# Converting float64 weights on the chip: from a float addition to an integer addition

## The chip, the cores and the metric

One core of a Trainium2 chip runs the whole program. Its engines are TensorE (PE, with its weight loads shown apart as PEld), VectorE (DVE), ScalarE (ACT), GpSimd (POOL) and SyncE (SP), which here only issues DMAs. The metric is the time of one execution in microseconds (us), the median of several runs.

## The reference

Three layers follow one another in float32. The weights of the second, `moe_w_in` and `moe_w_out`, are drawn in float32 and divided by a numpy scalar, and reach the kernel as float64.

```
a  = softmax over (keys within 16 of the query, and 24 block maxima + log 32)   # attention, 4 x 8 x 768 x 64
x  = (a @ [v, block means of v]) as 3072 tokens x 512
h  = x @ w_in                    # 512 x 2048, float64 in memory
x  = (h * cos(h)) @ w_out        # 2048 x 512, float64 in memory
logits = x @ phi                 # soft mixture: 8 experts x 4 slots
out = softmax_rows(logits) @ experts(softmax_columns(logits).T @ x)
```

## The kernel before

**Blocks and slots.** The 3072 tokens are six blocks of 512. The middle layer's 2048 hidden columns are sixteen tiles of 128. The main loop has a slot `s` for each hidden tile `f = s % 16` of each block, 96 slots. In a slot, `mm1` (L384 to L386) forms the hidden tile `h` with 12 products of 128 x 512, `act1` and `act2` (L400 to L411) turn it into `h cos h`, and `mm2` (L423 to L425), two slots later, adds 12 products to the block's four accumulators. Each float32 operand is split into a high part and a rest, so one product is three: `split_w` does so for the weights (L372 on ScalarE, L373 on GpSimd), L410 and L411 for the hidden tile, L362 and L363 for attention's result. The hidden tile has two places in PSUM, so slot `s + 2` writes over that of `s`, and must wait until L407 has read it.

**The cosine.** VectorE takes the hidden tile modulo one turn (L400, L401), ScalarE forms the sine of that (L402), VectorE multiplies (L407), ScalarE and GpSimd split (L410, L411).

**The weights.** A tile `f` of `w_in` and `w_out` together is 128 x 1024 float64 numbers, 1 MB as pairs of 32-bit words. `load_w(f)` brings it into `raw[f]`. There are two places for it (the first three tiles have a place more), so `load_w(f + 2)` waits on SP until all readers of `raw[f]` are done, and other loads stand behind it in SP's queue. Three steps then make the float32 tile `W[f]`, times 256, which stays in memory for all six blocks:

- `conv_1`: ScalarE multiplies the upper word, read as a float, by 2^-111 and takes its absolute value (L123).
- `conv_2`: VectorE shifts this three bits to the left (L134), puts in the sign (L135), takes the sign and exponent alone into a second tile `cv` (L137) and multiplies that by the lower word times 2^-52 (L138).
- `conv_3`: GpSimd adds `cv` to `W[f]` (L143).

The tile `cv` has two places by turns: one for odd `f` and one for even. Tiles 0 to 3 are converted ahead of the main loop, among the first block's attention (the tokens c0 to c3 of the string `PRE` say where). Tiles 4 to 15 are converted in slots 0 to 11, each three slots before its first split. So the conversion lies in the first block alone; the other five blocks find their weights ready.

**What sets the order.** Each engine runs its instructions in one order. The program is written out slot by slot, with attention's steps for later blocks put between (`at`, `at2`), and a planner that simulates a time line (`schedule_with_timeline_sim`) then fixes the order on each engine.

Of the kernel before, what the change touches and what calls it, by code (L numbers as in the profile page):

```python
# [23 lines left out]
QB = 64                      # queries per attention block  # L24
NQ = S // QB                 # 12 blocks per head
WIN, SUMB = 16, 32
KL = QB + 2 * WIN            # local keys of a block's window
NSUM = S // SUMB
KC = KL + NSUM               # key columns of a block: local and summary
NP = B * H // 2              # head pairs  # L30
TB = 512                     # tokens of a MoE block
# [37 lines left out]
SCALE = 1.0 / math.sqrt(D)    # a power of two  # L69
W_SCALE = 256.0              # the weights are held times this  # L70
TWO_PI = float(np.float32(2.0 * math.pi))
MAGIC = 12582912.0           # 1.5 * 2**23: adding and subtracting it rounds to an integer
# [3 lines left out]
def body(ctx: ExitStack, tc: tile.TileContext, q0, qk, kT, vn, vx, w, phi, ex, cst, out):  # L76
# [41 lines left out]
    def conv_1(f):  # L118
        """float64 words to the nearest float32, times 256: the upper word as a float, times 2^-111, has the
        exponent's offset adjusted; three bits to the left its exponent and 20 mantissa bits are in place;  # L120
        the sign follows, and the lower word is added as a float."""
        W[f] = wres.tile([128, 2, 512], F32, name=f"w{f}", tag=f"w{f}")
        nc.scalar.activation(W[f], raw[f][:, :, :, 1].bitcast(F32), AF.Abs, scale=2.0 ** -111)  # L123

    cvt = {}

    def conv_2(f):
        hw, lw = raw[f][:, :, :, 1], raw[f][:, :, :, 0]
        hw, lw = (x.rearrange("p a c -> p (a c)") for x in (hw, lw))
        wf = W[f].rearrange("p a c -> p (a c)")  # L130
        wi_ = wf.bitcast(I32)
        pool, tag = (wres, "w15") if f % 2 and f < 15 else (att, "cv")
        t = cvt[f] = pool.tile([128, 1024], F32, name=f"cv{f}", tag=tag, bufs=1)
        nc.vector.tensor_single_scalar(out=wi_, in_=wi_, scalar=3, op=ALU.logical_shift_left)  # L134
        nc.vector.scalar_tensor_tensor(out=wi_, in0=hw, scalar=-0x80000000, in1=wi_,  # L135
                                       op0=ALU.bitwise_and, op1=ALU.bitwise_or)
        nc.vector.tensor_single_scalar(out=t.bitcast(I32), in_=wi_, scalar=-0x00800000, op=ALU.bitwise_and)  # L137
        nc.vector.scalar_tensor_tensor(out=t, in0=lw.bitcast(U32), scalar=2.0 ** -52, in1=t,  # L138
                                       op0=ALU.mult, op1=ALU.mult)

    def conv_3(f):
        wf = W[f].rearrange("p a c -> p (a c)")
        nc.gpsimd.tensor_tensor(out=wf, in0=wf, in1=cvt.pop(f), op=ALU.add)  # L143

# [5 lines left out]
    def bank(name):  # L150
        """ahead of the main loop the accumulators' banks serve too"""
# [23 lines left out]
    def load_vb(b, i):  # L175
        """a third of a batch's values; the first batch's go into space that is not in use yet"""
# [12 lines left out]
    def vsum(b, i):  # L189
        """means of 32 keys: a pair's in its 32 rows"""  # L190
# [8 lines left out]
    def vsum_first():  # L199
        """the first batch's, all pairs in the rows that follow a window's keys"""  # L200
# [37 lines left out]
    def first_A(g, j):  # L238
        """scores of the first block's groups: the mask, times 8, is the last product of the sum"""
# [73 lines left out]
    def att_exps(g):  # L313
        """the same by row: the bias subtracts the maximum, the accumulator sums"""
# [6 lines left out]
    def att_norm(g, eng=None):  # L321
        # the hidden layer is formed in turns: x leaves attention divided by 2 pi
# [198 lines left out]
    def grab(pool, tag, units=1, **kw):  # L521
        """A freed place for expert weights: the next units are loaded there."""
# [38 lines left out]
    def fill(n):  # L561
        """products of no use: the tensor engine's clock halves when it idles"""
# [49 lines left out]
    for b in range(1, B):  # L612
        s = 8 * (3 * b - 2) - 4      # before the batch's first group
# [22 lines left out]
    def sched_m2(j, s):  # L636
# [4 lines left out]
        e = 2 * s + HF[1] + OX       # with the attention's exponentials  # L641
# [53 lines left out]
    def cT_mm(j):  # L695
        """the tokens' weights, transposed, four times"""
# [7 lines left out]
    def cT_split(j):  # L704
        """the high part and the rest, twice"""
# [63 lines left out]
    kept = []  # L769

    def release(u, want):
        """the place that an expert unit held goes to other use up to a number, else to the next units"""
# [36 lines left out]
    # the second products and the output by halves of the columns: the first half leaves while the second is formed  # L809
# [3 lines left out]
    for h in range(2):  # L813
# [23 lines left out]
        for i in range(NB):  # L837
            pool, tag, kw = places[(NB * h + i) % 4]
            o = pool.tile([128, 4, 256], F32, name=f"o{h}_{i}", tag=tag, **kw)
            for t in range(2):  # L840
# [7 lines left out]
                if i == 1:  # L848
                    before = slot_out, product   # what the other half's products leave room for
# [73 lines left out]
```

## Time and profile before

| | us |
|---|---|
| median of 3 runs | 809.73 (809.7 to 812.68) |
| span of the profiled execution, first to last instruction | 807.5 |
| TensorE busy in the span | 763.4 |
| VectorE busy | 516.0 |
| GpSimd busy | 465.7 |
| ScalarE busy | 422.0 |

The profile has one execution, with no time of its own beside its span. The median lies 2.2 us above that span. Busy time is the union of an engine's instructions; a group's sum over its instructions can be a little larger, since the end of one and the start of the next overlap. The mean granted clock of TensorE over the span is 0.976 of 2.4 GHz.

### The profile page before, as it was taken

The numbers are of one execution on the slowest core, as the hardware profiler recorded it, in microseconds if no ns is written. First come the engines' busy times: TensorE is split into PE (matmuls) and PEld (weight loads), VectorE is DVE, ScalarE is ACT, GpSimd is POOL, SyncE is SP. The second block draws the span as 40 slices with busy tenths as digits, with TensorE's granted clock in tenths as the row PEclk, the third lists the DMA queues.
The fourth block names the chain that finished last, engine by engine and source line by source line (L and its number), as shares of the span: only waits on it lengthen the run. The fifth ranks groups of instructions, "written<-read, shape, count | busy, mean of one in ns | idle before, by whom it ended". The sixth has DMA issues, their size and how long they took to land.

```text
span 807.5 us, 13934 instructions
## 1 busy us (share of the span) xinstructions
PE 763.4 (95%) x5517; PEld 590.9 (73%) x5517; DVE 516.0 (64%) x715; ACT 422.0 (52%) x774; POOL 465.7 (58%) x321
## 2 busy tenths in 40 slices
PE   9976788899999999999999999999999999999994
PEld 8865565667777877888778877778777888877453
DVE  5599999987746757557457369476476444433623
ACT  4839454754645645546537456565475454734212
POOL 1556999997655755745655646647547666562000
PEclk9997998999999999999999999999999999999998
DMA  9955555403233012011121110120000753227988
GB/s 317 308 159 212 218 177 181 168 25 109 68 99 105 3 52 72 25 63 64 52 63 38 50 56 21 50 76 25 25 1 27 275 195 102 79 88 277 364 308 271
DMA packets 34673, 98.30 MB, mean 122 GB/s; under 512 B 3376, under 2 KB 13744, under 8 KB 32560
## 3 DMA queue, kind: packets, MB, share of 16 engines
q1 hardware_dynamic: 34608, 97.42, 35.5%
q8 instruction: 43, 0.70, 0.4%
q14 instruction: 22, 0.18, 0.1%
HBM read 89.15 MB, written 6.29 MB: 118 GB/s over the span
## 4 chain that ended last, share of the span: by engine, by line
PE 68%; DVE 19%; ACT 5%; issue 4%; DMA 3%; POOL 0%; SPq 0%; ACTq 0%; DVEq 0%
PE h L384 9%; PE acc L423 9%; PE h L385 8%; PE acc L425 8%; PE h L386 8%; PE acc L424 8%; PE sc L286 3%; DVE w L135 3%; PE av L353 2%; DVE cv L137 2%; PE yp L822 2%; PE hp L789 2%; PE tr L335 2%; PE xt L449 2%; DVE cv L138 2%
## 5 line engine op out<-in xcount | busy, mean ns | idle before, releaser
L373 POOL TENSOR_TENSOR wol<-w,woh 128x512 fp32r<-128x512 f32 x96 | 141.4, 1473 | 100.5 <-ACT woh L372 100.4
L373 POOL TENSOR_TENSOR wil<-w,wih 128x512 fp32r<-128x512 f32 x96 | 136.1, 1418 | 71.7 <-ACT wih L372 71.7
L384 PE MATMUL h<-xh,wih 128*128 128x512 f32 x384 | 158.0, 411 | 13.9 <-DVE a L407 13.9
L411 POOL TENSOR_TENSOR gl<-a,gh 128x512 fp32r<-128x512 f32 x96 | 130.9, 1365 | 62.8 <-ACT gh L410 60.4
L385 PE MATMUL h<-xl,wih 128*128 128x512 f32 x384 | 155.3, 404 | 1.8 <-DVE xl L363 1.8
L386 PE MATMUL h<-xh,wil 128*128 128x512 f32 x384 | 154.9, 403 | 0.5 <-POOL wil L373 0.5
L423 PE MATMUL acc<-woh,gh 128*128 128x512 f32 x384 | 151.9, 402 | 0.5 <-DVE x L444 0.5
L425 PE MATMUL acc<-woh,gl 128*128 128x512 f32 x384 | 146.8, 399 | 5.2 <-POOL gl L411 5.2
L424 PE MATMUL acc<-wol,gh 128*128 128x512 f32 x384 | 150.6, 395 | 0.0
L400 DVE TENSOR_SCALAR a<-h 128x512 f32<-128x512 f32 x96 | 65.7, 685 | 85.5 <-PE h L386 81.6
L402 ACT ACTIVATE a<-a,halfpi 128x512 f32<-128x512 f32 x96 | 69.5, 724 | 96.2 <-DVE a L401 94.4
L372 ACT CAST wih<-w 128x512 fp32r<-128x512 f32 x96 | 59.3, 618 | 87.9 <-PE h L385 71.8
L407 DVE TENSOR_TENSOR a<-h,a 128x512 f32<-128x512 f32 x96 | 66.1, 689 | 59.3 <-ACT a L402 59.1
L384 PEld LDWEIGHTS h<-xh,wih 128*128 128x128 f32 x384 | 74.4, 194 | 32.8 <-DVE a L407 16.1
L425 PEld LDWEIGHTS acc<-woh,gl 128*128 128x128 f32 x384 | 71.9, 189 | 23.3 <-POOL gl L411 6.4
L385 PEld LDWEIGHTS h<-xl,wih 128*128 128x128 f32 x384 | 74.4, 194 | 17.7 <-DVE xl L363 2.3
L386 PEld LDWEIGHTS h<-xh,wil 128*128 128x128 f32 x384 | 74.2, 193 | 17.6 <-POOL wil L373 1.0
L423 PEld LDWEIGHTS acc<-woh,gh 128*128 128x128 f32 x384 | 72.0, 188 | 19.2 <-issue 2.7
L424 PEld LDWEIGHTS acc<-wol,gh 128*128 128x128 f32 x384 | 72.5, 189 | 16.1 <-issue 0.5
L410 ACT CAST gh<-a 128x512 fp32r<-128x512 f32 x96 | 59.4, 619 | 47.0 <-DVE a L407 46.3
L372 ACT CAST woh<-w 128x512 fp32r<-128x512 f32 x96 | 59.1, 616 | 19.3 <-PE acc L425 17.5
L401 DVE SCALAR_TENSOR_TENSOR a<-a,h 128x512 f32<-128x512 f32 x96 | 65.6, 683 | 2.3
(139 smaller groups left out, 1025.1 us busy)
## 6 DMA issues: line engine op xcount, KB each, us to landing
ex<-in_ex_dram SPq DMA_DIRECT2D x64, 512.0 KB
raw<-in_w_dram SPq DMA_DIRECT2D x16, 1024.0 KB
qk<-in_qk_dram SPq DMA_DIRECT2D x20, 736.0 KB
v<-in_vx_dram SPq DMA_DIRECT2D x24, 384.0 KB
kr<-in_kT_dram SPq DMA_DIRECT2D x16, 384.0 KB
vb<-in_vn_dram SPq DMA_DIRECT2D x12, 512.0 KB
out_dram<-o SPq DMA_DIRECT2D x12, 512.0 KB
v<-vs SPq DMA_DIRECT2D x40, 48.0 KB
```

The source lines that it names most:

```text
L372: nc.scalar.copy(hi, W[f][:, part, :])
L373: nc.gpsimd.tensor_tensor(out=lo, in0=W[f][:, part, :], in1=hi, op=ALU.subtract)
L384: nc.tensor.matmul(h, hi[:, c], xh[s // NF][:, t, :], start=t == 0, stop=False)
L385: nc.tensor.matmul(h, hi[:, c], xl[s // NF][:, t, :], start=False, stop=False)
L386: nc.tensor.matmul(h, lo[:, c], xh[s // NF][:, t, :], start=False, stop=t == 3)
L400: nc.vector.tensor_scalar(out=a, in0=h, scalar1=0.25, scalar2=MAGIC, op0=ALU.add, op1=ALU.add)
L402: nc.scalar.activation(a, a, AF.Sin, bias=halfpi, scale=-TWO_PI)
L407: nc.vector.tensor_tensor(out=a, in0=h, in1=a, op=ALU.mult)
L411: nc.gpsimd.tensor_tensor(out=gl, in0=a, in1=gh, op=ALU.subtract)
L423: nc.tensor.matmul(acc[t], gh[:, c], hi, start=f == 0, stop=False)
L424: nc.tensor.matmul(acc[t], gh[:, c], lo, start=False, stop=False)
L425: nc.tensor.matmul(acc[t], gl[:, c], hi, start=False, stop=f == NF - 1)
```

## The change

The lower word is no longer added as a float. ScalarE multiplies it by 2^-29, reads it as an unsigned integer and writes the product as a 32-bit integer. That integer is the number of units in the last place of the float32 tile, and adding it to the bits of the tile, as integers, gives the rounded number, with its carry into the exponent. So the second tile needs neither the exponent nor the product on VectorE: L137 and L138 go, ScalarE has a second instruction over 128 x 1024 in `conv_1`, and GpSimd's addition takes and gives 32-bit integers. The tile `cv` is now taken in `conv_1`, and written by ScalarE where VectorE wrote it. Comments are left out of the changed file too.

```diff
     def conv_1(f):
...
         W[f] = wres.tile([128, 2, 512], F32, name=f"w{f}", tag=f"w{f}")
+        pool, tag = (wres, "w15") if f % 2 and f < 15 else (att, "cv")
+        t = cvt[f] = pool.tile([128, 1024], I32, name=f"cv{f}", tag=tag, bufs=1)
         nc.scalar.activation(W[f], raw[f][:, :, :, 1].bitcast(F32), AF.Abs, scale=2.0 ** -111)
+        nc.scalar.mul(t, raw[f][:, :, :, 0].rearrange("p a c -> p (a c)").bitcast(U32), 2.0 ** -29)
...
     def conv_2(f):
-        hw, lw = raw[f][:, :, :, 1], raw[f][:, :, :, 0]
-        hw, lw = (x.rearrange("p a c -> p (a c)") for x in (hw, lw))
-        wf = W[f].rearrange("p a c -> p (a c)")
-        wi_ = wf.bitcast(I32)
-        pool, tag = (wres, "w15") if f % 2 and f < 15 else (att, "cv")
-        t = cvt[f] = pool.tile([128, 1024], F32, name=f"cv{f}", tag=tag, bufs=1)
+        hw = raw[f][:, :, :, 1].rearrange("p a c -> p (a c)")
+        wi_ = W[f].rearrange("p a c -> p (a c)").bitcast(I32)
         nc.vector.tensor_single_scalar(out=wi_, in_=wi_, scalar=3, op=ALU.logical_shift_left)
         nc.vector.scalar_tensor_tensor(out=wi_, in0=hw, scalar=-0x80000000, in1=wi_,
                                        op0=ALU.bitwise_and, op1=ALU.bitwise_or)
-        nc.vector.tensor_single_scalar(out=t.bitcast(I32), in_=wi_, scalar=-0x00800000, op=ALU.bitwise_and)
-        nc.vector.scalar_tensor_tensor(out=t, in0=lw.bitcast(U32), scalar=2.0 ** -52, in1=t,
-                                       op0=ALU.mult, op1=ALU.mult)
...
     def conv_3(f):
-        wf = W[f].rearrange("p a c -> p (a c)")
-        nc.gpsimd.tensor_tensor(out=wf, in0=wf, in1=cvt.pop(f), op=ALU.add)
+        wi_ = W[f].rearrange("p a c -> p (a c)").bitcast(I32)
+        nc.gpsimd.tensor_tensor(out=wi_, in0=wi_, in1=cvt.pop(f), op=ALU.add)
```

## Rows read from the trace of the kernel before

**Rows 1.** Busy time by stretch: length, then each engine, PEclk, DMA share, GB/s.

```profile
34.00:69.00 35.00, 24.10 (x262) 20.01 (x260) 32.50 (x35) 18.48 (x36) 20.20 (x9) 0.91 0.70 232
69.00:172.00 103.00, 87.04 (x494) 65.46 (x495) 101.40 (x101) 61.42 (x132) 91.75 (x44) 0.88 0.47 160
...
212.00:325.00 113.00, 112.18 (x761) 88.21 (x761) 74.58 (x107) 62.09 (x102) 65.01 (x49) 1.00 0.22 68
```

**Rows 2.** The chain that ended last, by engine.

```profile
PE 68%; DVE 19%; ACT 5%; issue 4%; DMA 3%; POOL 0%; SPq 0%; ACTq 0%; DVEq 0%
```

**Rows 3.** Groups of VectorE from 69 to 172 us: busy, mean ns, idle before.

```profile
L135 DVE SCALAR_TENSOR_TENSOR w<-raw,w 128x1024 int32<-128x1024 int32 x11 | 21.7, 1977 | 0.1
L138 DVE SCALAR_TENSOR_TENSOR cv<-raw,cv 128x1024 f32<-128x1024 uint32 x11 | 20.8, 1894 | 0.1
L137 DVE TENSOR_SCALAR cv<-w 128x1024 int32<-128x1024 int32 x11 | 14.8, 1346 | 0.1
L134 DVE TENSOR_SCALAR w<-w 128x1024 int32<-128x1024 int32 x10 | 13.4, 1344 | 0.0
```

**Rows 4.** The conversion's lines, whole span: shortest, median, longest in ns.

```profile
L134 DVE TENSOR_SCALAR w<-w x16: 641/1036/1834, 13.5 to 165.2; 128x1024 int32<-128x1024 int32 x16
L135 DVE SCALAR_TENSOR_TENSOR w<-raw,w x16: 1175/2119/2693, 15.9 to 166.5; 128x1024 int32<-128x1024 int32 x16
L137 DVE TENSOR_SCALAR cv<-w x16: 675/1186/2479, 17.7 to 168.8; 128x1024 int32<-128x1024 int32 x16
L138 DVE SCALAR_TENSOR_TENSOR cv<-raw,cv x16: 1171/1563/3274, 18.5 to 171.4; 128x1024 f32<-128x1024 uint32 x16
L143 POOL TENSOR_TENSOR w<-w,cv x16: 2341/2402/3397, 21.3 to 176.7; 128x1024 f32<-128x1024 f32 x16
L123 ACT ACTIVATE w<-raw x16: 1111/1160/1257, 11.1 to 163.1; 128x1024 f32<-128x1024 f32 x16
```

**Rows 5.** Groups of GpSimd from 69 to 172 us.

```profile
L143 POOL TENSOR_TENSOR w<-w,cv 128x1024 f32<-128x1024 f32 x10 | 27.7, 2769 | 2.4 <-DVE cv L138 2.4
L411 POOL TENSOR_TENSOR gl<-a,gh 128x512 fp32r<-128x512 f32 x11 | 21.2, 1934 | 3.8 <-ACT gh L410 3.8
L373 POOL TENSOR_TENSOR wil<-w,wih 128x512 fp32r<-128x512 f32 x10 | 19.1, 1913 | 1.8 <-ACT wih L372 1.8
L373 POOL TENSOR_TENSOR wol<-w,woh 128x512 fp32r<-128x512 f32 x9 | 17.0, 1887 | 2.4 <-ACT woh L372 2.4
L328 POOL TENSOR_TENSOR S<-S,rs 128x960 f32<-128x960 f32 x4 | 10.4, 2610 | 2.3 <-DVE rs L327 2.3
```

**Rows 6.** GpSimd in order of time, where VectorE leaves it alone: start, length.

```profile
31.66 1.79 POOL L328 TENSOR_TENSOR S<-S,rs 128x960 f32<-128x960 f32 x1 [2.28 <-DVE rs L327]
...
174.23 1.30 POOL L373 TENSOR_TENSOR wol<-w,woh 128x512 fp32r<-128x512 f32 x1
```

**Rows 7.** GpSimd and VectorE in order of time, from 90.48 us.

```profile
90.48 2.81 POOL L143 TENSOR_TENSOR w<-w,cv 128x1024 f32<-128x1024 f32 x1
91.10 3.27 DVE L138 SCALAR_TENSOR_TENSOR cv<-raw,cv 128x1024 f32<-128x1024 uint32 x1
93.26 2.24 POOL L411 TENSOR_TENSOR gl<-a,gh 128x512 fp32r<-128x512 f32 x1
```

**Rows 8.** TensorE in order of time, with the idle time ahead and its releaser.

```profile
42.90 1.15 PE L353 MATMUL av<-aT,v 120*64 120x64 f32 x32 [1.84 <-ACT aT L341]
...
53.89 0.51 PE L385 MATMUL h<-xl,wih 128*128 128x512 f32 x1 [1.78 <-DVE xl L363]
...
69.37 0.80 PE L384 MATMUL h<-xh,wih 128*128 128x512 f32 x1 [5.01 <-DVE a L407]
```

**Rows 9.** Groups of VectorE from 34 to 69 us.

```profile
L137 DVE TENSOR_SCALAR cv<-w 128x1024 int32<-128x1024 int32 x4 | 6.0, 1488 | 0.0
L138 DVE SCALAR_TENSOR_TENSOR cv<-raw,cv 128x1024 f32<-128x1024 uint32 x4 | 5.4, 1339 | 0.0
```

**Rows 10.** SP's waits up to 180 us: total, times, longest.

```profile
SPq L116 <- DVE cv L138: 72.8, 12, 10.4
```

## The prediction

> **What bounds the kernel now.** I read the stretches first. From 212 to 325 us, the second token block, TensorE is busy 112.18 of 113 us at full clock [rows 1]. Nothing done to VectorE can gain there, and the weights are converted by then. Between 69 and 172 us it is otherwise: TensorE 87.04 of 103 us at a granted clock of 0.88, VectorE 101.40 and GpSimd 91.75 [rows 1]. The chain of waits agrees: VectorE holds 19% of the span, some 153 us, TensorE 68% [rows 2].
>
> VectorE is not full of work of its own, though. The groups of that stretch give the four conversion passes 70.7 us (21.7 + 20.8 + 14.8 + 13.4) [rows 3]. Their shortest instances last 0.641, 1.175, 0.675 and 1.171 us (L134, L135, L137, L138) [rows 4], so 10, 11, 11 and 11 of them unhindered are 6.4 + 12.9 + 7.4 + 12.9 = 39.6 us. The other 31.1 us is stretch. GpSimd is stretched too: its groups sum to 95.4 us (27.7 + 21.2 + 19.1 + 17.0 + 10.4) [rows 5], while 10 adds of 2.341 [rows 4], 30 splits of 1.30 and 4 attention products of 1.79 [rows 6] are 23.4 + 39.0 + 7.2 = 69.6. Both engines' rows run longer, by 31.1 and 25.8 us. Three neighbouring rows show how: a GpSimd add runs from 90.48 to 93.29; VectorE's L138 starts at 91.10 and ends at 94.37, 1.08 after it; the next GpSimd split starts at 93.26 and ends at 95.50, 1.13 after that [rows 7]. Either engine waits for the other and then needs about its unhindered time. So VectorE's conversion passes and everything on GpSimd pass through one place by turns, and that place is what is full: 69.6 + 39.6 = 109.2 us of unhindered work in 103 us of time. What is over, 6%, must overlap.
>
> TensorE pays through the hidden tile's buffers: slot 2's first product sits idle 5.01 us for L407 of slot 0, which VectorE came to late [rows 8].
>
> **The change part by part.**
>
> *Two VectorE passes fewer (L137, L138).* In the stretch they are 14.8 + 20.8 = 35.6 us of busy time, 20.3 unhindered. VectorE goes to about 101.4 - 35.6 = 65.8 busy and stops being the tightest. GpSimd remains: what VectorE's 39.6 us did to it was 25.8, a factor of 0.65; the 19.3 that stay (6.4 + 12.9) do 12.6. Its rows then sum to 69.6 + 12.6 = 82.2, less 3.6 by which neighbouring rows overlap (95.4 in rows, 91.75 busy): 78.6. It idled 103 - 91.75 = 11.3 in the stretch, on VectorE and ScalarE alike; I keep half, 5.6. The stretch becomes 84.2 us and **18.8 us** are saved. A second way gives the same: the turns fall from 109.2 to 69.6 + 19.3 = 88.9, and 103 x 88.9 / 109.2 = 83.9. The ends: at best TensorE bounds. A mean clock of 0.88 means that 24% of 103 us, 24.7, ran at 1.2 GHz; at 2.4 that work takes 12.4 less, so 87.04 - 12.4 = 74.7, a saving of 28.3. At worst the 19.3 all land on GpSimd and it idles as before: 69.6 + 19.3 - 3.6 + 11.3 = 96.6, a saving of 6.4.
>
> Such turns are also a rule: the Trainium skill, page SBUF — State Buffer, section Who interferes with whom, says that GpSimd and VectorE share one port pair, that a VectorE instruction with two SBUF inputs or in a two-port mode contends for it, and that the other fully blocks. Taken strictly, the stretch after would last 88.9 us and save 14.1; the trace disagrees by 6%, for 109.2 us fitted into 103 [rows 1].
>
> *From 34 to 69 us.* There the two passes are 6.0 + 5.4 = 11.4 us [rows 9] of a VectorE busy 32.50 of 35 [rows 1]. Behind them queue the splits of attention's result (slot 0 waits 1.78 us for L363) and slot 0's cosine (the 5.01) [rows 8]. At best all 11.4 come back. Against it, ScalarE gets conversions 1 to 3 in addition, and it has queued work before slot 0: TensorE waits 1.84 us for its copy L341 [rows 8]. Three instructions of 1.15 are 3.4 us late at worst. Between +11.4 and -3.4, I take **6**, nearer the gain, because TensorE's two waits for VectorE are 6.8 us and its one for ScalarE 1.84. The very first conversion is hidden: slot 0 waits for attention then, not for a weight. ScalarE's new instruction costs 1.15 there if attention's exponentials queue behind it; I set it at nothing.
>
> *A second ScalarE instruction per conversion.* No row shows an integer product on ScalarE; the nearest is L123, same shape, same 8-byte step: 1.16 us in the median, 1.11 to 1.26 in all [rows 4]. I take 1.15. In the stretch ten of them bring ScalarE from 61.42 [rows 1] to 72.9 busy, 87% of 84.2: covered, but thinly. At twice that price, my upper end, it would be 84.4 and itself the bound, which is the second rival below. It brings one new wait: the integer tile lies in two places by turns, so ScalarE's product for f waits for GpSimd's add of f - 2, and behind it on ScalarE stand the splits, cosines and casts that GpSimd and TensorE need. That wait stood ahead of VectorE's L137 before. An add lies two slots ahead of the product that waits for it, so I count no more than the half of the idle time that stays.
>
> *Integers on GpSimd.* Same shape, two inputs, in place. No row has an integer add. From below: the product with a broadcast operand, 1.79 for 960 columns [rows 6], is 1.91 for 1,024. From above: two passes of the float add, 4.68. I take 2.34, the float add itself, the nearest in everything but type. Ten of them in the stretch make every 0.1 us worth 1 us: 4.3 us more saved at the lower end, 23.4 lost at the upper.
>
> *The loads.* The load of weight f + 2 waited on SP for L138, 72.8 us in 12 waits [rows 10], and other loads stand behind it. It will now wait for L135 and ScalarE's product, which come sooner. DMA is at 0.47 in the stretch [rows 1], so I cost this at nothing. The cover is thinner from 34 to 69 us, at 0.70 [rows 1].
>
> *The order.* The planner chooses each engine's order anew. From 212 us on there is 0.82 us of TensorE's idle time to win in a block [rows 1], and an unlucky order could lose a few; I set it at nothing.
>
> **The sum.** 807.5 - 18.8 - 6 = 782.7 us of span. The median of the runs, 809.73, lies 2.2 above the span, so **785 us**. Its own range, from half the two gains to some more of them, is 776 to 795.
>
> **The rivals.**
>
> *The integer add is slow (slower than before).* At 4.68 us, ten adds put 23.4 us on GpSimd: 84.2 + 23.4 = 107.6 against 103, and nothing is left of the first 6: about 814. It decides from about 4.2 us an add (18.8 / 10 above 2.34). For it: no row shows the type. Against: GpSimd's float work grows with the columns, 1.30 at 512 [rows 6] and 2.34 at 1,024 [rows 4], as if moving the data set it, and the data are as many. 0.15.
>
> *ScalarE is the new queue.* If each new 1.15 us delays the cosine or cast of its slot, 10 of them take 11.5 of the 18.8, and the first 6 vanish: 809.7 - 7.3 = 802. For it: 87% busy. Against: ScalarE's groups in the stretch idle for VectorE, and it was idle for 41.6 of 103 us [rows 1]. 0.10.
>
> *The turns are strict.* If nothing of the 88.9 us overlaps any more, 14.1 + 6 are saved: 790. For it: the three neighbours hardly overlap [rows 7]. Against: 109.2 in 103. 0.10.
>
> *Only VectorE's queue mattered.* If GpSimd is late merely because VectorE feeds it late, TensorE bounds at once: 28.3 + 11.4 saved, 770. For it: GpSimd idles 11.3 us waiting for the others. Against: GpSimd's own 69.6 + 12.6. 0.10.
>
> *The change shifts waits only*: the planner's new order eats the gain, 809. 0.04.
>
> **How the numbers follow.** The forecast has what remains, 0.51. Half a per cent, 4 us, is what a measurement here can tell from no change. Faster: 0.51 + 0.10 + 0.10 + 0.10 = 0.81. Within it: 0.04 and 0.04 of the slow add (an add of about 4.2 us) = 0.08. Slower: the other 0.11. The range runs from 768, the TensorE bound with 2 us to spare, to 804, which takes in the queue on ScalarE; the slow add and the shifted waits, 0.19, stay out.
>
> **What would show it.** Right: VectorE's lines of the conversion are L134 and L135 alone; GpSimd busier than VectorE in the stretch of slots 2 to 13, which lasts about 84 us; slot 2 starts near 63 instead of 69.4; from there on blocks of 112 to 113 us as before. Each step is wrong if: the integer add's shortest instance is not near 2.34; the new ScalarE instruction not near 1.15; VectorE's L135 stays stretched though GpSimd has fewer rivals. The prediction is wrong as a whole if the first block of slots does not shrink by some 25 us, or a later block grows.

## The result and the profile after

The changed kernel takes 798.25 us (median of four runs, 797.23 to 801.27) against 810.06 in the same comparison: a ratio of 0.985, 95% interval 0.9825 to 0.9871. It is faster by 12 us, where 25 were forecast, and its time lies in the range but 13 us above the forecast. The profiled execution spans 796.1 us against 807.5, so the comparison below accounts for 11.4 us. Of the six executions of e18, the profiled one was slow as a whole (1485 us) and is left out, so that run has a time but no rows. Line numbers after the conversion are lower by two in the new kernel: the integer add is L141, the passes L134 and L135, the new ScalarE product L126.

The page's chain of waits, by engine, stands against [rows 2]; VectorE fell from 19% to 12%, while DMA and ScalarE rose from 3% and 5% to 9% and 7%. Of DMA's share, 42.1 us lie ahead of slot 0 and 21.8 us between 93 and 121 us; three loads of weights are 15.2 of the latter.

```profile
PE 69%; DVE 12%; DMA 9%; ACT 7%; issue 2%; SPq 0%; ACTq 0%; DVEq 0%
```

Busy time by stretch, against [rows 1]: the time ahead of slot 2, then the stretch from slot 2's first product to slot 13's, then a later block. In before, slots 2 and 13 began at 69.37 and 171.76 us.

```profile
34.00:69.00 35.00, 26.97 (x281) 22.26 (x279) 30.99 (x32) 27.00 (x56) 20.41 (x11) 1.00 0.91 307
63.02:160.87 97.85, 83.01 (x509) 61.86 (x509) 74.33 (x82) 76.11 (x155) 80.90 (x46) 0.95 0.48 168
201.00:314.00 113.00, 112.48 (x767) 88.97 (x767) 73.61 (x108) 62.27 (x102) 65.80 (x49) 1.00 0.22 68
```

Slot 2 begins at 63.02, which is 6.35 us earlier. The stretch of slots 2 to 13 shrinks from 102.39 to 97.85, by 4.5 us only. Another 0.9 comes by slot 15, and from there all later slots lie 11.6 to 11.8 us earlier, with TensorE busy 112.48 of 113 as before. So the missing 13 us are all in that one stretch, and there no engine is full: TensorE 83.0, ScalarE 76.1, VectorE 74.3, GpSimd 80.9 of 97.85.

The stretch has two unlike parts. Here they are, parted where slot 9 begins, first before, then after the change:

```profile
69.37:135.76 66.39, 55.02 (x340) 41.22 (x340) 64.93 (x65) 35.37 (x70) 59.18 (x28) 0.91 0.52 176
135.76:171.76 36.00, 31.78 (x152) 24.04 (x153) 35.86 (x36) 25.44 (x61) 32.34 (x16) 0.83 0.36 126
...
63.02:133.45 70.43, 56.23 (x360) 41.16 (x361) 59.82 (x60) 54.98 (x109) 57.64 (x30) 0.95 0.59 208
133.45:160.87 27.42, 26.77 (x149) 20.70 (x149) 14.51 (x23) 21.13 (x47) 23.26 (x16) 0.94 0.18 65
```

Slots 2 to 8 became longer, 70.4 us against 66.4, and the rest shorter, 27.4 against 36.0. The work has moved forward: nine of GpSimd's adds start in the first part where seven did, and 24 of ScalarE's exponentials where 11 did. The last add starts at 141.6 us instead of 176.7. GpSimd's idle time lies mostly in the first part too, 12.8 us of 17.0.

The conversion's lines over the whole span, shortest, median and longest in ns, against [rows 4]:

```profile
L126 ACT ACTIVATE cv<-raw x16: 1116/1143/1264, 12.9 to 134.4; 128x1024 int32<-128x1024 uint32 x16
L134 DVE TENSOR_SCALAR w<-w x16: 642/1525/2923, 14.3 to 134.5; 128x1024 int32<-128x1024 int32 x16
L135 DVE SCALAR_TENSOR_TENSOR w<-raw,w x16: 1208/2195/3281, 16.3 to 135.7; 128x1024 int32<-128x1024 int32 x16
L141 POOL TENSOR_TENSOR w<-w,cv x16: 2348/2388/2830, 17.7 to 141.6; 128x1024 int32<-128x1024 int32 x16
```

The two unknown prices came out as taken: 1.14 us for the integer product on ScalarE and 2.35 for the integer add. The passes that stay are stretched more than before: the shift's median went from 1.04 to 1.53 us, the sign's from 2.12 to 2.20.

GpSimd's groups from 63.02 to 160.87 us, against [rows 5]; behind the bar stand busy us, the mean of one in ns, and the idle time ahead with what ended it.

```profile
L141 POOL TENSOR_TENSOR w<-w,cv 128x1024 int32<-128x1024 int32 x10 | 24.8, 2478 | 3.6 <-issue 2.4 <-ACT w L125 1.2
L409 POOL TENSOR_TENSOR gl<-a,gh 128x512 fp32r<-128x512 f32 x12 | 19.3, 1610 | 6.9 <-ACT gh L408 6.9
L371 POOL TENSOR_TENSOR wil<-w,wih 128x512 fp32r<-128x512 f32 x11 | 16.2, 1473 | 3.1 <-ACT wih L370 3.1
L371 POOL TENSOR_TENSOR wol<-w,woh 128x512 fp32r<-128x512 f32 x9 | 14.4, 1604 | 3.8 <-ACT woh L370 3.8
L326 POOL TENSOR_TENSOR S<-S,rs 128x960 f32<-128x960 f32 x4 | 8.1, 2036 | 0.4 <-DVE rs L325 0.4
```

These rows sum to 82.8 us, against 95.4 before: GpSimd did get shorter. What did not shrink is its idle time. In the right-hand column it is 17.8 us (11 to 13 before), and 15.0 of it ended with something from ScalarE (8.0 before, [rows 5]). The largest piece is one wait, seen in the two engines' order of time. GpSimd:

```profile
60.79 1.26 POOL L371 TENSOR_TENSOR wil<-w,wih 128x512 fp32r<-128x512 f32 x1
68.94 1.28 POOL L409 TENSOR_TENSOR gl<-a,gh 128x512 fp32r<-128x512 f32 x1 [6.88 <-ACT gh L408]
```

ScalarE, over the same time:

```profile
63.16 1.12 ACT L126 ACTIVATE cv<-raw 128x1024 int32<-128x1024 uint32 x1
64.30 1.28 ACT L316 ACT_TABLE_LOAD   x1
65.59 0.40 ACT L316 ACTIVATE S<-S,mx 128x120 f32<-128x120 f32 x1
...
68.26 0.60 ACT L408 CAST gh<-a 128x512 fp32r<-128x512 f32 x1
```

GpSimd's next instruction in its order is the subtraction that needs the cast, and the cast stands on ScalarE behind a conversion's product, a table load and seven exponentials of attention. ScalarE in its turn waits for VectorE. Three of its groups in the stretch of 63.02 to 160.87 us:

```profile
L316 ACT ACTIVATE S<-S,mx 128x120 f32<-128x120 f32 x32 | 12.2, 382 | 4.3 <-DVE mx L295 4.3
...
L400 ACT ACTIVATE a<-a,halfpi 128x512 f32<-128x512 f32 x12 | 8.7, 722 | 4.2 <-DVE a L399 4.0
L408 ACT CAST gh<-a 128x512 fp32r<-128x512 f32 x12 | 7.4, 617 | 2.2 <-DVE a L405 2.2
```

That is 10.5 us for VectorE, whose conversion passes are long beside GpSimd's rows. Every engine works in its own order, and in this stretch each of the three waits for another's. ScalarE waits less than before, though: it idled 41.6 us of 102.4 then and 21.7 of 97.9 now.

### The profile page after: what moved, and what is told of

The parts are those of the page before. It is cut to its first block, busy times and chain, and to the rows that moved or that the text cites. A ratio compares the mean times of both kernels' runs of the same rounds, so it can differ in the third digit from the quotient of the medians.

```text
span 796.1 us, 13916 instructions
## 1 busy us (share of the span) xinstructions
PE 759.4 (95%) x5517; PEld 588.2 (74%) x5517; DVE 477.1 (60%) x683; ACT 438.2 (55%) x790; POOL 448.0 (56%) x321
## 4 chain that ended last, share of the span: by engine, by line
PE 69%; DVE 12%; DMA 9%; ACT 7%; issue 2%; SPq 0%; ACTq 0%; DVEq 0%
PE h L382 9%; PE acc L421 9%; PE acc L423 9%; PE h L383 9%; PE acc L422 8%; PE h L384 8%; DMA kr<-in_kT_dram 4%; PE sc L284 4%; PE av L351 3%; PE yp L820 2%; DMA raw<-in_w_dram 2%; PE hp L787 2%; PE tr L333 2%; PE xt L447 2%; ACT S L316 2%
## 5 line engine op out<-in xcount | busy, mean ns | idle before, releaser
L371 POOL TENSOR_TENSOR wol<-w,woh 128x512 fp32r<-128x512 f32 x96 | 139.4, 1452 | 106.4 <-ACT woh L370 106.3
L371 POOL TENSOR_TENSOR wil<-w,wih 128x512 fp32r<-128x512 f32 x96 | 130.9, 1364 | 74.6 <-ACT wih L370 73.9
L382 PE MATMUL h<-xh,wih 128*128 128x512 f32 x384 | 155.9, 406 | 10.3 <-DVE a L405 10.3
L409 POOL TENSOR_TENSOR gl<-a,gh 128x512 fp32r<-128x512 f32 x96 | 127.8, 1331 | 64.1 <-ACT gh L408 64.1
L421 PE MATMUL acc<-woh,gh 128*128 128x512 f32 x384 | 150.1, 404 | 4.9 <-ACT gh L408 4.4
L383 PE MATMUL h<-xl,wih 128*128 128x512 f32 x384 | 152.9, 398 | 1.6 <-DVE xl L361 1.6
L384 PE MATMUL h<-xh,wil 128*128 128x512 f32 x384 | 152.4, 397 | 0.0
L422 PE MATMUL acc<-wol,gh 128*128 128x512 f32 x384 | 148.8, 395 | 0.0
L398 DVE TENSOR_SCALAR a<-h 128x512 f32<-128x512 f32 x96 | 65.8, 685 | 95.4 <-PE h L384 89.8
L400 ACT ACTIVATE a<-a,halfpi 128x512 f32<-128x512 f32 x96 | 69.5, 724 | 86.2 <-DVE a L399 84.3
L405 DVE TENSOR_TENSOR a<-h,a 128x512 f32<-128x512 f32 x96 | 66.2, 689 | 65.8 <-ACT a L400 65.8
L382 PEld LDWEIGHTS h<-xh,wih 128*128 128x128 f32 x384 | 72.8, 190 | 30.0 <-DVE a L405 13.3
L421 PEld LDWEIGHTS acc<-woh,gh 128*128 128x128 f32 x384 | 72.5, 189 | 24.1 <-ACT gh L408 5.3
L383 PEld LDWEIGHTS h<-xl,wih 128*128 128x128 f32 x384 | 72.8, 190 | 16.9 <-DVE xl L361 2.2
L399 DVE SCALAR_TENSOR_TENSOR a<-a,h 128x512 f32<-128x512 f32 x96 | 65.7, 684 | 2.4
```

The costliest lines, as they stand in the source:

```text
L371: nc.gpsimd.tensor_tensor(out=lo, in0=W[f][:, part, :], in1=hi, op=ALU.subtract)
L382: nc.tensor.matmul(h, hi[:, c], xh[s // NF][:, t, :], start=t == 0, stop=False)
L383: nc.tensor.matmul(h, hi[:, c], xl[s // NF][:, t, :], start=False, stop=False)
L384: nc.tensor.matmul(h, lo[:, c], xh[s // NF][:, t, :], start=False, stop=t == 3)
L398: nc.vector.tensor_scalar(out=a, in0=h, scalar1=0.25, scalar2=MAGIC, op0=ALU.add, op1=ALU.add)
L400: nc.scalar.activation(a, a, AF.Sin, bias=halfpi, scale=-TWO_PI)
```

## The experiments

Theories were named by what they hold responsible for the missing us. G: GpSimd's length with the turns. T: the sum of the turn work. V: the time for which VectorE is occupied. A (and S): ScalarE's queue. E: the conversions coming too early. O: the planner's order alone. L: the length of single pieces. All runs are edits of the changed kernel; e15 alone edits the one before. The table ahead of the details gives each run's median, its ratio to the kernel before, the start of slot 2, the length of slots 2 to 13 (from slot 2's first product to slot 13's), and the busy time of VectorE and GpSimd within it. The last four columns come from the one profiled execution, up to 2.5 us off the median. A length that begins with a later slot 2 also holds less work, since other work was done ahead of it; where that matters, the text goes by the time at which slot 13 begins.

| run | us | ratio [95%] | slot 2 | slots 2 to 13 | VectorE | GpSimd |
|---|---|---|---|---|---|---|
| before | 810 | | 69.4 | 102.4 | 100.8 | 91.5 |
| after | 798.25 | 0.985 [0.983, 0.987] | 63.0 | 97.9 | 74.3 | 80.9 |
| e1 no product | 794.88 | 0.981 [0.978, 0.984] | 66.4 | 95.0 | 73.9 | 86.2 |
| e2 no add | 785.89 | 0.970 [0.966, 0.974] | 62.4 | 85.4 | 61.9 | 55.1 |
| e3 product twice | 797.29 | 0.983 [0.980, 0.987] | 67.5 | 89.8 | 62.5 | 80.7 |
| e4 CL of 2 (the same program) | 798.70 | 0.985 [0.982, 0.988] | 63.3 | 97.8 | 74.4 | 80.9 |
| e5 no passes, no add | 786.47 | 0.970 [0.968, 0.972] | 64.9 | 85.1 | 37.1 | 50.4 |
| e6 no passes | 786.24 | 0.970 [0.968, 0.972] | 66.1 | 84.7 | 37.0 | 71.3 |
| e7 split on VectorE | 797.70 | 0.984 [0.981, 0.986] | 71.7 | 89.0 | 72.5 | 65.7 |
| e8 CP of 1 (the same program) | 798.48 | 0.984 [0.982, 0.986] | 65.2 | 98.0 | 72.9 | 81.0 |
| e9 no shift | 789.30 | 0.973 [0.970, 0.976] | 64.1 | 89.2 | 57.2 | 79.7 |
| e10 no sign | 784.28 | 0.968 [0.965, 0.970] | 65.4 | 80.9 | 49.3 | 71.8 |
| e11 add in halves | 798.15 | 0.985 [0.981, 0.989] | 62.0 | 101.4 | 75.9 | 83.5 |
| e12 add and passes in halves | 803.00 | 0.990 [0.988, 0.993] | 68.9 | 98.9 | 77.7 | 80.8 |
| e13 rounding on ScalarE | 803.86 | 0.992 [0.989, 0.995] | 69.6 | 94.4 | 65.0 | 80.6 |
| e14 fewer splits | 789.83 | 0.975 [0.971, 0.978] | 61.5 | 90.5 | 70.7 | 68.4 |
| e15 before, rounding on ScalarE | 819.18 | 1.011 [1.008, 1.013] | 69.9 | 108.0 | 101.9 | 95.2 |
| e16 reductions for passes | 794.22 | 0.979 [0.977, 0.982] | 75.0 | 80.5 | 65.0 | 70.9 |
| e17 shift in steps | 797.30 | 0.984 [0.981, 0.987] | 61.6 | 97.9 | 74.3 | 80.9 |
| e18 no add, whole conversion | 789.37 | 0.972 [0.970, 0.975] | | | | |

**e1 and e3: ScalarE's product left out, or done twice.**

```diff
-        nc.scalar.mul(t, raw[f][:, :, :, 0]..., 2.0 ** -29)      # e1: GpSimd adds one zero tile
+        nc.scalar.mul(t, raw[f][:, :, :, 0]..., 2.0 ** -29)      # e3: the line twice
```

> The changed kernel without ScalarE's integer product: GpSimd adds one tile of zeros, filled once by VectorE, so the lower words are left out and nothing else. Theory S (the new instruction stands in ScalarE's queue ahead of cosines and casts): ten instructions of 1.15 us leave slots 2 to 13, which shrink from 97.9 to about 86 us, and the kernel takes 785 to 789 us. Theory E (weights are converted sooner than they are needed, since their places come free sooner, and crowd slots 2 to 9): nothing is gained, or loads come sooner still; 796 to 800. Theory G (GpSimd and VectorE's two passes by turns are the bound): GpSimd's work is the same; 795 to 799.

> The changed kernel with ScalarE's integer product formed twice into the same tile. Theory S: each of ten further instructions of 1.15 us delays a cosine or cast in slots 2 to 13, and 3 more stand ahead of slot 0: 806 to 812 us. Theory G and theory E: ScalarE has 22 us of idle time in the stretch and takes them: 798 to 802.

Without the product 3.4 us come back, and the two intervals just overlap; with two of them the time is the same, although ScalarE's part of the stretch goes up to 81.9 of 89.8 us. ScalarE's added instruction is not what keeps the 13 us.

**e2: the add left out.**

```diff
-        nc.gpsimd.tensor_tensor(out=wi_, in0=wi_, in1=cvt.pop(f), op=ALU.add)
+        cvt.pop(f)
```

> The changed kernel without GpSimd's integer addition: the lower words are left out, while ScalarE still forms its product. Theory G: ten additions of 2.35 us leave slots 2 to 13, VectorE's L134 and L135 lose their stretch (37.5 us in rows against 18.5 unhindered), and the stretch comes near TensorE's 75 to 80 us: 776 to 782 us in all. Theory S: ScalarE's queue is as it was, and at most a few us of gain are seen: 793 to 798. Theory E: the crowding costs nothing if it brings no work to GpSimd, so as G, 778 to 786.

12.4 us come back, and the two passes lie near their unhindered time, the shift at 0.69 us in the median instead of 1.53, the sign at 1.23 instead of 2.20:

```profile
L134 DVE TENSOR_SCALAR w<-w x16: 640/685/1926, 14.1 to 122.2; 128x1024 int32<-128x1024 int32 x16
L135 DVE SCALAR_TENSOR_TENSOR w<-raw,w x16: 1212/1226/2693, 16.2 to 123.4; 128x1024 int32<-128x1024 int32 x16
```

In the stretch the two passes sum to 25.7 us instead of 37.5, where 18.5 is unhindered, so the adds make up most of what stretches them. These are adds of earlier tiles, for a tile's own add waits for its passes. The time lies above G's figure and at the upper end of E's.

**e4 and e8: meant as the same work elsewhere.** CL, the number of slots by which a conversion leads as written, from 4 to 2; and CP from 0 to 1, which writes a slot's conversion behind its second activation and product.

> The changed kernel with each conversion, and the load behind it, written two slots later in the main loop (one slot ahead of its first split instead of three). Theory E: the conversions spread over slots 2 to 13 again, slots 2 to 9 take less than 70 us, and the kernel gains 5 to 12: 786 to 793 us. Theory G: the same work passes in the same stretch, 795 to 800. Theory S: the same instructions stand in ScalarE's queue, 795 to 800, more if a split now waits for its weight.

> The same work; a slot's conversion is written after its second activation and second product instead of ahead of them, so the planner orders all engines anew. Theory O (where each row falls in the planner's order is worth several us by itself): the time moves by 3 us or more either way. Theories G and A: the same work in the same slots, 796 to 800 us.

Neither edit reached the chip. The planner put everything back: on each of the engines, the DMA issues included, the traces of e4 and e8 have the changed kernel's instructions, one by one in the same order. So the two are repeats, 798.70 and 798.48, and E and O stay untested. The rows speak for E rather than against it: the conversions do run ahead, and slots 2 to 8 last longer than before (70.4 against 66.4 us).

**e5 and e6: VectorE's passes left out, with the add and without it.**

```diff
-        nc.vector.tensor_single_scalar(out=wi_, in_=wi_, scalar=3, op=ALU.logical_shift_left)
-        nc.vector.scalar_tensor_tensor(out=wi_, in0=hw, scalar=-0x80000000, in1=wi_, ...)
-        nc.gpsimd.tensor_tensor(out=wi_, in0=wi_, in1=cvt.pop(f), op=ALU.add)    # e5 alone
```

> Left out: both VectorE passes of the conversion (L134, L135) and GpSimd's integer add, so the weights hold unfinished words; ScalarE's two instructions and the loads stay. Theory G (the turns of VectorE's passes and GpSimd's rows keep slots 2 to 13 long): the turn work of those slots falls from 88.9 us to the splits and attention products alone, 46.2 us, so TensorE bounds, and the stretch goes to 78 to 82 us; with the 85.4 us of the run without the add as the step before, that is 779 to 783 us. Theory A (ScalarE's chain of exponentials, table loads, copies and conversions sets the stretch): nothing is gained over the run without the add, 784 to 788 us.

> Left out: VectorE's two passes of the conversion (L134, L135); GpSimd's integer add and ScalarE's product stay. Theory G: GpSimd's rows lose their stretch of 10.5 us, and the turn work falls by 19.3 us, as much as the adds alone would take away by 23.4; so about 788 us (786 to 791), near the run without the add. If GpSimd's own length is the bound without any turns (theory G2: its 80 us busy and the idle time it keeps), the stretch falls only by the 10.5 at most and by little else: 793 to 798 us. Theory A: no change, 796 to 799 us.

All three of e2, e5 and e6 end at 786 us, with slots 2 to 13 in 85. Whichever partner of the turns goes, nearly the whole of the missing gain comes back, and when both go it is no more. So 12 us hang on the two working side by side; e16 below asks how much of that is the turns. For e5, G's figure was too low, and the time lies in A's range; e6 lies in G's and rules out A's. What is behind the 786 us no run shows. TensorE is the fullest engine there, busy 77.6 of 84.7 us in e6, ScalarE 70.6.

Two things went along in these runs and were not parted from the turns. The planner orders all engines anew whenever a pass or an add goes. And a weight's place comes free sooner, so that the next load starts sooner: SP waits 51.2 us for L135 in the changed kernel, and 24.4 us in e2. More waiting for loads is not by itself slower: ScalarE idles 5.5 us for weights in slots 2 to 13 of the changed kernel, 6.3 in e2 and 8.0 in e14, which are both faster.

**e9 and e10: one pass left out.** L134 alone, L135 alone.

> Left out: VectorE's shift (L134, one input, 0.64 us unhindered, 1.5 in the median); the sign pass (L135, two inputs, 1.18 unhindered) and GpSimd's integer add stay. Taking out both passes gave 786.2 us, 12 less. Theory T (both passes take turns with GpSimd by their unhindered length): a third of the turn work of the passes goes, so 4 us come back, 794 us. Theory P (only the pass with two inputs hinders GpSimd): 797 to 799 us. Theory L (what costs is the length of a single stretched piece, not the sum): the longest pieces stay, 797 to 799 us.

> Left out: VectorE's sign pass (L135, two inputs, 1.18 us unhindered, 2.2 in the median); the shift (L134, one input) and GpSimd's integer add stay. Theory T: two thirds of the 12 us come back, 790 us. Theory P: nearly all of it, 786 to 787 us. Theory L: what is left on VectorE is short, 786 to 789 us. If even the shift alone keeps GpSimd and VectorE apart: 795 us or more.

9 and 14 us come back, more than any theory's figure. The shift is worth more than the 6.4 us that ten of them last unhindered. The sign pass alone is worth as much as both, if not 2 us more (the intervals overlap), so what the passes cost does not add up pass by pass. The window of e9 shows where its gain comes from:

```profile
64.12:153.32 89.20, 81.91 (x499) 61.91 (x498) 57.22 (x70) 72.06 (x151) 79.74 (x47) 0.95 0.51 174
```

GpSimd is busy 79.7 us, as much as after the change (80.9); its idle time fell from 17.0 to 9.5 us.

**e11, e12 and e17: other pieces, the same work.** The add in two halves of 512 columns; the add and both passes so; the shift in steps of two words.

```diff
+        for c in (slice(0, 512), slice(512, 1024)):
+            nc.gpsimd.tensor_tensor(out=wi_[:, c], in0=wi_[:, c], in1=t[:, c], op=ALU.add)
...     # e17:
+        ws = wi_.rearrange("p (c t) -> p t c", t=2)
+        nc.vector.tensor_single_scalar(out=ws, in_=ws, scalar=3, op=ALU.logical_shift_left)
```

> The same work; GpSimd's integer add in two halves of 128x512, some 1.2 us each, so that a split or another engine's row can go in between. Theory L (the slot's chain of VectorE, ScalarE and GpSimd stands behind one long piece at each step; the sum of the turns would fit): 3 to 6 us come back, 792 to 795 us. Theory T (the sum of the turn work): nothing, 797 to 800 us, the fixed cost of 13 more instructions included.

> The same work; GpSimd's integer add and both VectorE passes in halves of 128x512. Theory L: 5 to 9 us come back, 789 to 793 us, more than with the add alone in halves. Theory T: nothing, or some us lost to the fixed cost of 39 more instructions: 798 to 803 us.

> The same work; VectorE's shift (L134) goes through the tile in steps of two words, first the even, then the odd ones. Its shortest instance should go from 0.64 to about 1.1 to 1.2 us, the time of a row that reads one word a cycle. Theory T with the turns bound to the fast way of reading: the shift is no longer stretched (median near its shortest, instead of 1.5), GpSimd no longer waits for it, and some 3 to 8 us of the 9 come back that leaving it out gave: 790 to 795 us. If the turns do not depend on the way of reading: the longer pass costs 10 x 0.5 us more, 799 to 804 us.

Halves gain nothing and, on both engines, cost 5 us: it isn't the length of one piece. (The four times of e11 lie at 795.6 and at 801, and its profile is one of the longer two.) The shift in steps runs exactly as before, in its shortest and median instance:

```profile
L135 DVE TENSOR_SCALAR w<-w x16: 647/1526/2930, 13.7 to 133.2; 128x1024 int32<-128x1024 int32 x16
```

So e17 tells nothing about the way of reading. It has the order of the changed kernel too, and serves as a third repeat, 1 us from it.

**e7: nine of GpSimd's subtractions of the stretch (13 in all) moved to VectorE.**

```diff
+        eng = nc.vector if part and f in first else nc.gpsimd
...
+        eng.tensor_tensor(out=lo, in0=W[f][:, part, :], in1=hi, op=ALU.subtract)
```

> The same work, with the low half of the second weight's split (L371 wol) of the first 13 weights moved from GpSimd to VectorE. In slots 2 to 13 these are nine rows of 14.4 us on GpSimd, against some 0.7 us each on VectorE if it does a two-input subtraction of 512 columns like L405. Theory G: the turn work falls by 9 x 0.6 = 5.4 us and GpSimd by 14.4, so 4 to 8 us come back: 790 to 794 us. Theory A: no change, 797 to 799 us. Against it: the split stands behind VectorE's queue, and TensorE's second products wait for it, 800 us or more.

By the total a miss for G: 797.7, no change, as A had it. Slots 2 to 13 take 89.0 us instead of 97.9, but slot 2 begins 8.7 us later, and slot 13 at the same time (160.7 against 160.9). So the shorter stretch is no gain: work lies ahead of slot 2 instead of behind it, and eight of the stretch's 32 exponentials and one of its ten adds are gone from it. From 34 to 69 us VectorE is busy 33.07 us, against 30.99 after the change:

```profile
34.00:69.00 35.00, 26.47 (x282) 22.58 (x277) 33.07 (x32) 26.04 (x64) 22.15 (x11) 0.92 0.83 290
```

**e13 and e15: VectorE relieved, ScalarE loaded.** In slots 0 to 11 ScalarE rounds, and VectorE takes one instruction instead of two; in the changed kernel and in the one before.

```diff
+        elif s < 12:
...
+            nc.scalar.activation(ai, h, AF.Identity, bias=quarter)      # ai: a as whole numbers
+            nc.vector.tensor_tensor(out=a, in0=ai, in1=h, op=ALU.subtract)
         else:
             nc.vector.tensor_scalar(out=a, in0=h, scalar1=0.25, scalar2=MAGIC, op0=ALU.add, op1=ALU.add)
...
```

> The same work; in slots 0 to 11 the rounding for the cosine takes one VectorE instruction instead of two: ScalarE writes the hidden tile plus 0.25 as a whole number, and VectorE subtracts. That takes 12 rows of 0.68 us, 8.2 us, off VectorE (L398) and puts 12 of about 0.6 on ScalarE; GpSimd's rows stay as they are. Theory V (VectorE's queue is still the bound): 4 to 8 us come back, 790 to 794 us. Theory G (GpSimd's length is the bound): no change, 797 to 799 us. Theory A (ScalarE's chain): slower, 800 to 805 us, for ScalarE gets 7 us more and a step in each slot's chain.

> The kernel before, with its four VectorE passes for each weight, and the rounding of slots 0 to 11 as in e13. VectorE is busy 100.8 of 102.4 us in slots 2 to 13 there. Theory V: 12 rows of 0.68 us fewer give 6 to 9 us, 801 to 804 us. Theory G: GpSimd is busy 91.5 of 102.4 us and stays so; no change, 809 to 811 us. Theory A: slower, 811 us or more.

Slower by 5.6 and by 9 us, as A alone had it. Moving 0.68 us of VectorE's time to ScalarE is a loss even where VectorE is busy 100.8 of 102.4 us, as in before. V, in its plain form, falls here: in e15 VectorE stays busy 101.9 us, of a stretch that grew to 108.0. Why it is a loss is argued, not shown. The instructions that were moved read PSUM and are not stretched (L398 lasts 0.67 to 0.69 us in all 96 instances after the change), and a slot's chain changes engines once more.

**e14: GpSimd relieved, VectorE untouched.** The subtractions that e7 moved are left out.

> Left out: GpSimd's subtraction for the low half of the second weight's split (L371 wol) of the first 13 weights; TensorE multiplies with the high half in its place, as often as before. In slots 2 to 13 these are nine rows of 14.4 us on GpSimd; VectorE's work stays. Theory G: 8 to 12 us come back, 786 to 790 us. Theory V: only what the missing rows stretched VectorE by, some 3 us of its 18, comes back: 794 to 797 us. If the turns count by their sum (theory T): 13 x 1.3 of 88.9 us go, about 9 us come back, 788 to 791 us.

8.4 us come back, as G and T say, although VectorE is nearly as busy in the stretch as after the change (70.7 us against 74.3). With all adds in place the sign pass is at its unhindered time here, 1.23 us in the median, and the shift longer, 1.83, so which of the passes is stretched is not fixed.

**e16: VectorE occupied without turns.** Three reductions in place of the two passes.

```diff
+        for i in range(3):
+            nc.vector.reduce_max(out=m, in_=wf, axis=AX.X)
```

> Left out: VectorE's two passes of the conversion (L134, L135), so the weights hold unfinished words. In their place VectorE reduces the same 128x1024 tile three times to its maximum: one input, about 1.23 us each by the 128x960 reduction of attention (L295), which lasts 1.13 to 1.15 us in all 20 instances and is never stretched. VectorE stays occupied as long as by the two passes in the median (3.7 us for each weight), and GpSimd's add waits for it as before. Theory T (GpSimd and VectorE take turns, and their sum is what counts): no turns with the conversion any more, 785 to 789 us, as with the passes left out. Theory V (the time that VectorE is occupied): 796 to 800 us, as after the change. Between the two both would count.

The 48 reductions are never stretched, and slots 2 to 13 are as short as in any run:

```profile
L137 DVE TENSOR_REDUCE rm<-w x48: 1164/1208/1220, 13.7 to 119.4; 128x1 f32<-128x1024 f32 x48
```

```profile
75.02:155.51 80.49, 77.04 (x496) 60.70 (x497) 64.95 (x83) 63.23 (x126) 70.88 (x48) 0.97 0.45 155
```

But the stretch is short in part because work moved ahead of it: slot 2 begins 12 us later, and 22 of the 48 reductions, 26.6 us, lie ahead of it, where the passes ahead of it took 19.8. Slot 13 begins 5.4 us earlier than after the change, and 10.1 earlier in e6. By the total, 794.2, a third of the missing gain comes back. So both count, as the last sentence of the expectation had it. Without turns with the passes, but with VectorE occupied as long (57.9 us for the 48 reductions, 57.2 for the 32 passes), 4 us of 12 come back; the other 8 went with VectorE's time, or with the new order. That time is itself long because the passes are stretched, 57.2 us against 29.6 unhindered, so the 8 us are no proof against the turns. A run with turn-free work as short as the unhindered passes would part the two; there is none. The Trainium skill, page SBUF — State Buffer, section Who interferes with whom, says that a reduction on VectorE never contends with GpSimd on this chip; the trace agrees, with 1.22 us at most in 48.

**e18: the whole conversion without an add.** The product is scaled so that VectorE's first pass can put it in place, and GpSimd has no part in the conversion.

```diff
-        nc.scalar.mul(t, ..., 2.0 ** -29)
+        nc.scalar.mul(t, ..., 2.0 ** -29 * 0.935)
-        nc.vector.tensor_single_scalar(out=wi_, in_=wi_, scalar=3, op=ALU.logical_shift_left)
+        nc.vector.scalar_tensor_tensor(out=wi_, in0=wi_, scalar=3, in1=cvt.pop(f),
+                                       op0=ALU.logical_shift_left, op1=ALU.bitwise_or)
-        nc.gpsimd.tensor_tensor(out=wi_, in0=wi_, in1=cvt.pop(f), op=ALU.add)
```

> The whole conversion with no GpSimd instruction: ScalarE's product is scaled to whole numbers from 0 to 7, so that VectorE's first pass can put them in place of the three bits that its shift leaves empty ((w << 3) | low); the sign pass follows. The weights are then float32 values within one unit of the last place instead of the nearest ones. The turn work of slots 2 to 13: ten adds of 2.35 us go, ten VectorE passes get a second input, 1.2 instead of 0.64 us; 88.9 - 23.4 + 5.5 = 71 us. Theory T (the sum of the turns, down to the bound of TensorE with its own waits, at about 785): 785 to 788 us, near the run without the add. Theory V (VectorE's time): 5.5 us more than the run without the add, 790 to 793 us. Theory A (ScalarE's chain): 786 us too, for ScalarE's part is as in that run.

789.4 us (786.08 to 791.02), 2.8% under the kernel before and some 1.3% under the changed one (0.972 against 0.985, intervals apart). It lies between T's figure and V's, 3.5 us above the run without the add.

## Why the prediction was right and wrong

**Slot 2 earlier by 6 us: right.** It was 6.35, and slot 2 began at 63.02 where "near 63" stood. Slots 0 and 1 begin just 0.3 and 0.1 us earlier, so nothing came by L363, the first of the two paths named. By the second, slot 0's cosine, slot 2's wait fell from 5.01 to 2.28 us; where the other 3.6 us came from is open. GpSimd is busier than VectorE in the stretch, as said, and the later blocks are as before.

**ScalarE's product 1.15 and the integer add 2.34: right**, at 1.14 and 2.35 in the table of lines above. The rival of the slow add is out, and ScalarE as the new queue is out as the main cause: e1 gives back 3.4 us of 13, e3 costs nothing. ScalarE's queue as a whole is not out: A alone foresaw e5, e13 and e15.

**The stretch of 84.2 us, 18.8 saved: wrong, and this is the whole miss.** At 97.85 it lies beyond even the end called "at worst", 96.6. It was made of GpSimd's 78.6 us busy and "half" of its idle time, 5.6. Busy came out at 80.9, so the forecast was 2.3 too low: the stretch now holds 32 splits where it counted 30, 2.6 us of work. Idle came out at 97.85 - 80.90 = 17.0: **the step that halved the idle time failed**, and is 11.4 of the 13.7 us by which the stretch was too short. The reasoning was that GpSimd idles for VectorE and ScalarE alike, so that a lighter VectorE would end its share. In fact the idle time grew, and it now ends with ScalarE's results 15.0 us of 17.8, behind exponentials and table loads as at 62 to 69 us. ScalarE is at least in part a link: it idles 10.5 us for VectorE itself, and GpSimd's idle time falls to 9.5 us when nothing but the shift is taken off VectorE (e9). Why the idle time grew is open beyond that. The forecast also took the stretch as one even piece, and the conversions and exponentials crowd into its first part.

**That the turns bind: right in part.** Removing either partner gives the missing gain (e2, e6, e10), and the passes lie near their unhindered time in the median once the adds are gone (e2). But filling VectorE with work that takes no turns gives only a third of it (e16). The rival of strict turns had 88.9 us for the stretch; it lasted 9 us longer, so turns alone do not make its length. **Their size was read wrongly.** The second way of the forecast scaled the stretch with the sum of the turns, 103 x 88.9 / 109.2 = 83.9. Take the same sum for the runs, 88.9 less what each leaves out at its unhindered length: ten adds in e2 (65.5), both passes in e6 (69.6), ten sign passes of 1.21 in e10 (76.8), ten shifts in e9 (82.5). The stretch is 81 to 85 us in the first three, 89 in e9, 98 after the change, and 102 before it, at 109.2. Counted by the start of slot 13 it is 146 to 151 us, 153, 161 and 172. So there is a floor, a steep part above it, and then a flatter one: of the 20.3 us that the change took away, 10.9 came back by slot 13, and of the next 6.4 (e9) 7.6.

**VectorE 65.8 us busy: too low**, 74.3. The two passes that stay got longer, 1.98 to 2.24 us and 1.34 to 1.51 in the mean, 37.5 us in all where 35.1 were counted. That is 2.4 of the 8.5. Another part is the arithmetic: 35.6 us of rows were taken from a busy time of 101.4, in which rows overlap each other, so less busy time went than the rows' sum. The stretch also holds a few more rows of the slots' cosines.

**TensorE as the bound, 770 us: its size was wrong.** The floor of the runs is 784 to 786 us: TensorE keeps 3.6 to 7.6 us of idle time in slots 2 to 13 (e10, e2) and is busy 77 to 79 us there instead of 74.7, and slot 2 still begins at 62 to 66 us. **The loads and the planner's order at nothing: not tested.** e4, e8 and e17 ran in the changed kernel's own order and say only that the time repeats within 1 us.

What stays open: e10 and e14 have the same sum of turns, 77 (nine subtractions of 1.30 fewer in e14), and differ by 9.6 us in slots 2 to 13 and by 5.5 in all, so the sum is no law; and how much of the remaining 17 us of idle time is ScalarE's exponentials was not tried by itself. Nor was it tried whether the conversions come too early, what the planner's order is worth, or what e7 gives behind slot 2 alone.

## What to carry to other kernels

Where two engines take turns at one place, shortening one partner need not shorten the stretch: add up what either is busy and what it is idle, and treat the idle time as something that must be shown to go, not as a share that goes along. What is taken off first can be worth less than what is taken off next: here the two passes of VectorE that the change took out were worth 12 us together, and after them the add on GpSimd was worth 12 and the sign pass 14 by itself. Compare runs at a common point, such as the start of slot 13, and not by the length of a stretch alone: e7's stretch was 9 us shorter and e16's 17, but slot 13 began 0.2 and 5.4 us earlier. And see in the trace that an edit has moved anything, for e4 and e8 came out as the same program.

## What was not expected of the hardware

VectorE's reductions of 128x1024 lasted 1.16 to 1.22 us beside GpSimd's adds, where the shift of the same tile, 0.64 unhindered, lasted up to 2.92. The shift in steps of two words cost no more than the one in order (0.647 against 0.642 us). Integers cost what floats cost: 1.14 us for uint32 to int32 on ScalarE at a step of 8 bytes, 2.35 for the add on GpSimd, and 1.26 to 1.29 for its half, so that a half costs some 0.1 more than half.
